# Packed attention and a gated feed-forward on one core: the output product with its operands exchanged, and 64 leftover tokens of each batch kept for later

## The chip, the cores and the metric

The kernel runs on one core of a Trainium2 chip. The metric is the time of one execution on the device in microseconds (us). The core has a matrix engine (TensorE, PE in the profile; its weight loads are PEld), VectorE (DVE), ScalarE (ACT), GpSimd (POOL) and a queue engine (SyncE, SP) from which most transfers are issued. A matmul holds one operand in the array, the stationary one (up to 128 x 128, brought by a weight load), and streams the other, the moving one, column by column through it; its result lands in PSUM, which has eight banks of 512 float32 a partition.

## The reference

```python
# q, k, v: (8 batches, 8 heads, 576 tokens, 64); p: (8, 8, 32, 64)
def sm_attn(qq, kk, vv):
    s = 0.125 * qq @ kk.transpose(0, 1, 3, 2)
    a = np.exp(s - s.max(-1, keepdims=True))
    return (a / (a.sum(-1, keepdims=True) + 1e-9)) @ vv
packed = sm_attn(p, k, v)
attn = sm_attn(q, packed, packed)
x = attn.transpose(0, 2, 1, 3).reshape(4608, 512)
h = x @ w_in                      # w_in 512 x 2048, float64 in memory
g = h * erf(softplus(h))
out = g @ w_out                   # w_out 2048 x 512, float64 in memory
```

## The kernel before

Each batch of 576 tokens goes through attention, then through the feed-forward. The 2048 columns of w_in (rows of w_out) are 16 tiles f of 128. Large products are done in three terms with float32r operands split in a high and a low part: high x high, high x low, low x high.

**Attention** (`attention`, a generator of 12 stages) loads p, k, v, q, makes the first softmax a1 and the packed values pt, then the second softmax, whose high and low halves are `a2[b]`. The chunks of k, v and q share the `kvq` buffers (6 of 128 x 576). **W'** (`w_prime`, L248) multiplies pt with 512 columns of w_in, so that the h product runs from the softmax directly; tiles `wph` and `wpl`, four buffers each.

**Weights** arrive as float64: `load_f32` (L77) stages 128 x 512 words of 8 bytes in one of two buffers `wst` and converts them with one ACT and three DVE instructions (L88 to L91). The third to eighth of these loads borrow `wpl` and `wph` buffers (`EARLY`, L56). `split_w_out` makes the high and low part of each of the 16 w_out tiles.

**Units.** A unit before is (batch b, half c of its tokens, block i of two f tiles): 8 x 2 x 8 = 128 units. `h_block` (L284) computes two f tiles of h by 288 tokens, 12 matmuls with W' stationary and the 288 tokens moving (L297), copies them out of PSUM on ACT (L301, L303) and makes the gate. The first 32 units take softplus and erf in groups of three units with a table load on ACT for each (`gate_group`); the others use a formula of tanh and square on ACT (L311 to L316) and three DVE instructions (L314, L315, L317). `split_g` (L263) makes g's high and low part `gh`, `gl` on DVE (L266, L267), two buffers each. `o_block` (L323) then adds the unit's share of the output: 24 matmuls with 128 x 128 blocks of w_out stationary and 288 tokens of g moving (L337), into four banks `ps_o0` to `ps_o3`, one for each 128 output columns, holding the output transposed. At the end of a (batch, half) the banks are copied out on ACT (L344) and written to `outT`, which the host transposes.

**Order.** Batches 0 and 1 go through in two turns of eight f tiles each (`TURNS`), so that the second half of the weights may come later; their second turn adds to the output in memory by an accumulating transfer from POOL (L347). The loop at the end of the function emits, for each unit n, its h product, the items planned for n (attention stages, W', conversions), and the out product of unit n - 3 (`LAG`; n - 5 in the first 32). A scheduler with a simulated timeline then sets the order on each engine, where instructions run strictly in that order. Attention of batch 1 is planned over units 1 to 6, that of batch b + 2 over the first six units after batch b; each W' tile is planned as soon as a buffer of four is free.

Of the kernel before, what the change touches and what calls it, by code (L numbers as in the profile page):

```python
# [27 lines left out]
@with_exitstack  # L28
def tile_pack_attention_moe(ctx: ExitStack, tc: tile.TileContext, qT, kT, v, pT, w_in, w_out, outT):
    nc = tc.nc  # L30
# [4 lines left out]
    HT = S // 2  # L35
    NDM = DM // P
    FB = 512
    NFB = DFF // FB
    NBLK = DFF // (2 * P)
    NT = S // P  # L40
# [5 lines left out]
    G = 3  # L46
    GROUPED = 4 * NBLK
    LAG_G = 5
    NB0 = 2
    TURNS = (0, NBLK // 2, NBLK)  # L50
    WI_AT = (-1, 1)
# [73 lines left out]
    def attention(b, roomy=False):  # L125
# [5 lines left out]
        def chunk(name, tag="kvq"):  # L131
            if tag == "kvq":
                return apool.tile([P, S], F32, name=f"{name}_{b}", tag="kvq", bufs=6)[:]
            return tpool.tile([P, S], F32, name=f"{name}_{b}", tag=tag)[:]
# [18 lines left out]

        p = apool.tile([P, NC, NK], F32, name=f"p{b}", tag="p")
        nc.sync.dma_start(p[:], pT[b])
# [72 lines left out]
        blocks = ta[:].rearrange("p r (n k) -> p (r n) k", k=NK)  # L228
        mx = apool.tile([P, 4 * nb], F32, name=f"mx{b}", tag="mx")
        wide = mx[:].unsqueeze(2).to_broadcast([P, 4 * nb, NK])  # L230
# [31 lines left out]

    def split_g(hs, b, c, i):  # L263
        ghi = tpool.tile([P, 2, HT], F32R, name=f"gh{b}_{c}_{i}", tag="gh", bufs=2)
        glo = tpool.tile([P, 2, HT], F32R, name=f"gl{b}_{c}_{i}", tag="gl", bufs=2)
        nc.vector.tensor_copy(ghi[:], hs[:])  # L266
        nc.vector.tensor_tensor(glo[:], hs[:], ghi[:], op=ALU.subtract)  # L267
        gs[b, c, i] = (ghi, glo)

    def gate_group():  # L270

        ts = []
        for hs, b, c, i in group:
            t = tpool.tile([P, 2, HT], F32, name=f"t{b}_{c}_{i}", tag="t0")
# [4 lines left out]
        for t, (hs, b, c, i) in zip(ts, group):  # L279
            nc.vector.tensor_tensor(hs[:], t[:], hs[:], op=ALU.mult)  # L280
            split_g(hs, b, c, i)
        group.clear()

    def h_block(b, c, i, n):  # L284

        grouped = n < GROUPED
        hs = tpool.tile([P, 2, HT], F32, name=f"hs{b}_{c}_{i}", tag="t1" if grouped and n // G % 2 else "hs")
        for k in range(2):
            f = (2 * i + k) * P
            j, fo = f // FB, f % FB  # L290
            whi, wlo = wp[b, j]
            ps = ps_h.tile([P, 512], F32, name=f"h{b}_{c}_{i}_{k}", tag="ps_h")
            m = 0
            ahi, alo = a2[b]
            for r in range(2):
                for w, a in ((whi, ahi), (whi, alo), (wlo, ahi)):
                    nc.tensor.matmul(ps[:, 0:HT], w[:, r, fo:fo + P], a[:, r, c * HT:(c + 1) * HT],  # L297
                                     start=(m == 0), stop=(m == 5))
                    m += 1
            if grouped:  # L300
                nc.scalar.copy(hs[:, k, :], ps[:, 0:HT])  # L301
            else:
                nc.scalar.mul(hs[:, k, :], ps[:, 0:HT], 0.5)  # L303
        if grouped:
            group.append((hs, b, c, i))
            if len(group) == G or n == GROUPED - 1:
                gate_group()
            return
        t = tpool.tile([P, 2, HT], F32, name=f"t{b}_{c}_{i}", tag="t0")
        u = tpool.tile([P, 2, HT], F32, name=f"u{b}_{c}_{i}", tag="t1")  # L310
# [7 lines left out]
        split_g(hs, b, c, i)  # L318

    acc = {}  # L320
    begun = set()

    def o_block(b, c, i, first, last):  # L323

        g = gs.pop((b, c, i))
        t0 = b * S + c * HT
        if first:
            acc[b, c] = []
            for d in range(NDM):
                po = ps_o.tile([P, 512], F32, name=f"o{b}_{c}_{i}_{d}", tag=f"ps_o{d}")  # L330
                acc[b, c].append(po)
        for d in range(NDM):
            for k in range(2):
                f = 2 * i + k
                terms = [(wo_hi, g[0]), (wo_hi, g[1]), (wo_lo, g[0])]
                for n, (w, gg) in enumerate(terms):
                    nc.tensor.matmul(acc[b, c][d][:, 0:HT], w[f][:, d * P:(d + 1) * P], gg[:, k, :],  # L337
                                     start=(first and k == 0 and n == 0),
                                     stop=(last and k == 1 and n == len(terms) - 1))
        if not last:  # L340
            return
        for d in range(NDM):
            ob = tpool.tile([P, HT], F32, name=f"ob{b}_{c}_{i}_{d}", tag="ob", bufs=NDM)
            nc.scalar.copy(ob[:], acc[b, c][d][:, 0:HT])  # L344
            where = outT[d * P:(d + 1) * P, t0:t0 + HT]
            if (b, c) in begun:
                nc.gpsimd.dma_start(where, ob[:], accum_op=ALU.add)  # L347
            else:
                nc.sync.dma_start(where, ob[:])
        begun.add((b, c))  # L350


    segs = [(b, c, i0, i1) for i0, i1 in zip(TURNS, TURNS[1:]) for b in range(NB0) for c in range(2)]
    segs += [(b, c, 0, NBLK) for b in range(NB0, B) for c in range(2)]
    units = [(b, c, i, i == i0, i == i1 - 1) for b, c, i0, i1 in segs for i in range(i0, i1)]
    first_use, last_of, uses, last_use = {}, {}, [], {}
    for n, (b, c, i, _, _) in enumerate(units):
        first_use.setdefault(b, n)
        last_of[b] = n
        if (b, i // 2) not in last_use:  # L360
            uses.append((b, i // 2))
        last_use[b, i // 2] = n

# [6 lines left out]
    conv = {}  # L370
    for i in range(NBLK):
        ph = max(n for n, start in enumerate(TURNS) if i >= start)
        items = []
        if i % 2 == 0:
            items += [("wi", i // 2, c) for c in range(4)]
        items += [("wo", 2 * i), ("wo", 2 * i + 1)]
        conv.setdefault(ph, []).append(items)
    for ph, lists in conv.items():
# [4 lines left out]
        else:  # L383
            flat = [it for items in lists for it in items]
            n0, n1 = (2 * NB0 * TURNS[p] for p in (ph - 1, ph))
            for k, it in enumerate(flat):
# [19 lines left out]
    for k, (b, j) in enumerate(uses):  # L406
        if b not in ready:
            plan_attention(b)
        n = ready[b]
        if k >= NFB:  # L410
            n = max(n, last_use[uses[k - NFB]])
# [4 lines left out]
    for f in range(DFF // P):  # L416
        made = max(n for n, its in plan.items() if ("wo", f) in its)
# [39 lines left out]
    do(early[4:])  # L457
    behind = 0
    for n in range(len(units) + LAG):
        if n < len(units):  # L460
            grouping[0] = n < GROUPED
            h_block(*units[n][:3], n)
            do(plan.pop(n, []))
        while behind <= n - (LAG_G if n < GROUPED else LAG):
            o_block(*units[behind])
            behind += 1

# [37 lines left out]
```

## Time and profile before

| what | value |
|---|---|
| runs | 804.53, 797.12, 798.9 us; median 798.9 |
| profiled execution | span 795.2 us from the first to the last instruction; no separate time is given for it |
| TensorE busy | 742.5 us (93%), 6352 matmul instructions |
| weight loads busy | 669.1 us (84%) |
| DVE, ACT, POOL busy | 571.2 (72%), 582.7 (73%), 15.0 us (2%) |
| mean granted TensorE clock | 0.961 |
| transfers | 58.41 MB, mean 73 GB/s |

The matmuls are pipelined: the duration of one in the profile is its way through the array, and the distance between two starts is what it costs in a stream. The granted clock is given as a share of full speed. In a group's row, after the names and shapes and the count, stand the busy time in us, the mean duration of one in ns, and the idle time of the engine before them with what ended it.

### The profile page before, as it was taken

What the parts mean: (1) busy time and instruction counts of PE and PEld (TensorE: products, weight loads), DVE (VectorE), ACT (ScalarE), POOL (GpSimd) and SP (SyncE); (2) the same over time, 40 slices, a digit from 0 to 9 for tenths busy, and PEclk for the clock granted to TensorE, in tenths of its full rate; (3) what the DMA queues carried; (4) which work ended last, traced back from release to release, by engine and by line L of the source; (5) the groups of instructions that cost most, each with busy time, mean ns of one, the idle gap of its engine ahead of it and who ended that gap; (6) DMA issues with size and microseconds to landing.
All of it is one profiled execution on the core that took longest, in us unless ns stands there. A gap on an engine that the chain in (4) does not pass through costs nothing.

```text
span 795.2 us, 15330 instructions
## 1 busy us (share of the span) xinstructions
PE 742.5 (93%) x6352; PEld 669.1 (84%) x6352; DVE 571.2 (72%) x876; ACT 582.7 (73%) x974; POOL 15.0 (2%) x22
## 2 busy tenths in 40 slices
PE   3469858999999999999999999999999999999998
PEld 1248636899888899899888998899988999899998
DVE  3897787753386669767886769767786769776664
ACT  3368368868577778778687867888688877888784
POOL 0000000000111200000000000000000000000000
PEclk8559879999999999999999999999999999999999
DMA  9714633321441431002300221002400210000000
GB/s 312 279 58 154 216 130 114 102 65 48 106 87 13 94 84 57 31 2 82 132 31 1 82 76 57 32 1 79 132 31 1 70 54 2 31 1 31 2 31 31
DMA packets 31814, 58.41 MB, mean 73 GB/s; under 512 B 3584, under 2 KB 14848, under 8 KB 31744
## 3 DMA queue, kind: packets, MB, share of 16 engines
q1 hardware_dynamic: 29440, 55.06, 21.1%
q0 software_dynamic: 2304, 2.36, 2.4%
q8 instruction: 50, 0.82, 0.4%
q14 instruction: 20, 0.16, 0.1%
HBM read 45.61 MB, written 11.80 MB: 72 GB/s over the span
## 4 chain that ended last, share of the span: by engine, by line
PE 83%; ACT 6%; DVE 5%; DMA 5%; issue 1%; SPq 0%; ACTq 0%
PE o L337 49%; PE h L297 25%; PE wp L254 4%; PE p L209 2%; DMA wi<-w_in 2%; DMA q<-qT 1%; DMA wos<-w_out 1%; PE s L223 1%; PE s L176 1%; PE t L197 1%; ACT t L275 1%; ACT L278 1%; ACT t L278 1%; ACT a L185 1%; DMA p<-pT 1%
## 5 line engine op out<-in xcount | busy, mean ns | idle before, releaser
L337 PE MATMUL o<-gh,woh 128*128 128x288 f32 x1024 | 301.4, 301 | 4.0 <-ACT woh L104 2.9
L337 PE MATMUL o<-gl,woh 128*128 128x288 f32 x1024 | 301.6, 296 | 0.6 <-DVE gl L267 0.6
L337 PE MATMUL o<-gh,wol 128*128 128x288 f32 x1024 | 300.7, 296 | 0.0
L337 PEld LDWEIGHTS o<-gh,woh 128*128 128x128 f32 x1024 | 190.3, 188 | 32.8 <-DVE t L314 8.1
L337 PEld LDWEIGHTS o<-gh,wol 128*128 128x128 f32 x1024 | 192.5, 189 | 6.4 <-issue 6.0
L337 PEld LDWEIGHTS o<-gl,woh 128*128 128x128 f32 x1024 | 192.9, 188 | 1.3 <-DVE gl L267 0.9
L297 PE MATMUL h<-a2h,wph 128*128 128x288 f32 x512 | 155.2, 304 | 15.7 <-ACT a2h L243 10.4
L297 PE MATMUL h<-a2l,wph 128*128 128x288 f32 x512 | 154.4, 302 | 2.2 <-DVE a2l L244 2.2
L297 PE MATMUL h<-a2h,wpl 128*128 128x288 f32 x512 | 154.5, 302 | 0.4 <-DVE wpl L257 0.4
L303 ACT ACTIVATE hs<-h 128x288 f32<-128x288 f32 x192 | 78.1, 412 | 80.3 <-PE h L297 77.2
L297 PEld LDWEIGHTS h<-a2h,wph 128*128 128x128 f32 x512 | 98.5, 193 | 27.6 <-ACT a2h L243 13.9
L317 DVE SCALAR_TENSOR_TENSOR hs<-t,hs 128x576 f32<-128x576 f32 x96 | 72.5, 755 | 60.4 <-ACT t L316 60.4
L297 PEld LDWEIGHTS h<-a2h,wpl 128*128 128x128 f32 x512 | 99.0, 193 | 3.4 <-issue 2.7
L297 PEld LDWEIGHTS h<-a2l,wph 128*128 128x128 f32 x512 | 98.8, 193 | 3.4 <-DVE a2l L244 2.9
L267 DVE TENSOR_TENSOR gl<-hs,gh 128x576 fp32r<-128x576 f32 x128 | 96.4, 753 | 1.9
L266 DVE CAST gh<-hs 128x576 fp32r<-128x576 f32 x128 | 58.4, 456 | 47.5 <-PE o L337 46.3
L316 ACT ACTIVATE t<-t,bias 128x576 f32<-128x576 f32 x96 | 74.0, 771 | 23.0 <-DVE t L315 22.7
L314 DVE SCALAR_TENSOR_TENSOR t<-t,hs 128x576 f32<-128x576 f32 x96 | 71.8, 748 | 13.0 <-ACT u L313 12.8
L311 ACT ACTIVATE t<-hs,bias 128x576 f32<-128x576 f32 x96 | 74.5, 776 | 2.2
L312 ACT ACTIVATE t<-t,bias 128x576 f32<-128x576 f32 x96 | 74.3, 774 | 1.9
L313 ACT ACTIVATE u<-t,bias 128x576 f32<-128x576 f32 x96 | 74.5, 776 | 1.5
L315 DVE SCALAR_TENSOR_TENSOR t<-u,t 128x576 f32<-128x576 f32 x96 | 72.3, 753 | 1.2
(65 smaller groups left out, 661.8 us busy)
## 6 DMA issues: line engine op xcount, KB each, us to landing
k<-kT SPq DMA_DIRECT2D x32, 288.0 KB, 4.3
q<-qT SPq DMA_DIRECT2D x32, 288.0 KB, 4.3
outT<-ob SPq DMA_DIRECT2D x64, 144.0 KB, 1.8
wi<-w_in SPq DMA_DIRECT2D x16, 512.0 KB, 5.9
v<-v SPq DMA_DIRECT2D x32, 256.0 KB, 3.6
wos<-w_out SPq DMA_DIRECT2D x16, 512.0 KB, 4.1
outT<-ob POOLq DMA_DIRECT2D x16, 144.0 KB, 4.5
v<-v SPq DMA_DIRECT2D x8, 128.0 KB, 4.5
```

The costliest lines, as they stand in the source:

```text
L266: nc.vector.tensor_copy(ghi[:], hs[:])
L267: nc.vector.tensor_tensor(glo[:], hs[:], ghi[:], op=ALU.subtract)
L297: nc.tensor.matmul(ps[:, 0:HT], w[:, r, fo:fo + P], a[:, r, c * HT:(c + 1) * HT], start=(m == 0), stop=(m == 5))
L303: nc.scalar.mul(hs[:, k, :], ps[:, 0:HT], 0.5)
L311: nc.scalar.activation(t[:], hs[:], AF.Tanh, bias=bias[:, 0:1], scale=2.0 * T_SCALE)
L312: nc.scalar.activation(t[:], t[:], AF.Square, bias=bias[:, 1:2], scale=Q_SCALE)
L313: nc.scalar.activation(u[:], t[:], AF.Tanh, bias=bias[:, 2:3], scale=U_SCALE)
L314: nc.vector.scalar_tensor_tensor(t[:], t[:], 0.5 * A2, hs[:], op0=ALU.mult, op1=ALU.add)
L315: nc.vector.scalar_tensor_tensor(t[:], u[:], 0.5 * A1, t[:], op0=ALU.mult, op1=ALU.add)
L316: nc.scalar.activation(t[:], t[:], AF.Tanh, bias=bias[:, 3:4], scale=2.0 * A_SCALE)
L317: nc.vector.scalar_tensor_tensor(hs[:], t[:], 1.0, hs[:], op0=ALU.add, op1=ALU.mult)
L337: nc.tensor.matmul(acc[b, c][d][:, 0:HT], w[f][:, d * P:(d + 1) * P], gg[:, k, :], start=(first and k == 0 and n == 0), stop=(last and k = ...
```

## The change

The operands of the output product change places. For each f tile and each 128 tokens of a batch, g's 128 x 128 block is now stationary and 512 columns of w_out are moving, so the result is 128 tokens by all 512 output columns, a full bank, no longer transposed. A unit is one f tile by the whole batch of 576 tokens: still 128 units, with 12 h matmuls and the same gate on 128 x 576. 576 tokens are four tiles of 128 and 64 left over. `split_g` copies the 64 left tokens of gh and gl on GpSimd into tiles kept for a pair of batches (`rest`: 4 f tiles x 2 batches x 64 tokens each), and `o_rest` computes them as one full tile of 128 tokens after the pair's second batch: 4 groups of 12 matmuls in bank `ps_o0`. For the last pair these groups are put between and behind the last units' out products, in a bank of attention. A unit's first out product takes the banks in the order 1, 2, 3, 0.

To make room, `kvq` has five buffers instead of six, p and mx one instead of two, W' three instead of four, the borrowed staging buffers (`EARLY`) are four instead of six; `ob` has three of 128 x 512 instead of four of 128 x 288. The turns of batches 0 and 1, the lags, the planned units of attention and of the conversions keep their numbers; with the new units, a W' tile is used by four units in a row and f tile n is needed at unit n of a turn, where before two were needed at each of the first four units.

```diff
-    opool = ctx.enter_context(tc.tile_pool(name="wo", bufs=2 * (DFF // P) + 1))
+    opool = ctx.enter_context(tc.tile_pool(name="wo", bufs=2 * NF + 1))
...
-    EARLY = ("wpl", "wpl", "wph", "wph", "wpl", "wpl")
+    EARLY = ("wpl", "wpl", "wph", "wph")
...
-    wpool = ctx.enter_context(tc.tile_pool(name="wp", bufs=NFB))
+    rpool = ctx.enter_context(tc.tile_pool(name="rest", bufs=NFB))
+    wpool = ctx.enter_context(tc.tile_pool(name="wp", bufs=NW))     # NW = 3
...
+        pair, k = b // 2, f // PER
+        if (pair, k) not in rest:
+            rest[pair, k] = [rpool.tile([P, PER, 2, TAIL], F32R, name=f"{x}{pair}_{k}", tag=x) for x in ("rh", "rl")]
+        for kept, g in zip(rest[pair, k], (ghi, glo)):
+            nc.gpsimd.tensor_copy(kept[:, f % PER, b % 2, :], g[:, NTB * P:S])
...
+    def terms(g, f):
+        return ((g[0], wo_hi[f]), (g[1], wo_hi[f]), (g[0], wo_lo[f]))
+
+    def o_block(b, f, first, last):
+        g = gs.pop((b, f))
+        order = range(NTB)
+        if first:
+            order = [*range(1, NTB), 0]
+            acc[b] = [ps_o.tile([P, 512], F32, name=f"o{b}_{f}_{x}", tag=f"ps_o{x}") for x in range(NTB)]
+        for x in order:
+            for n, (gg, w) in enumerate(terms(g, f)):
+                nc.tensor.matmul(acc[b][x][:], gg[:, x * P:(x + 1) * P], w[:], start=(first and n == 0),
+                                 stop=(last and n == 2))
+        if not last:
+            return
+        for x in range(NTB):
+            ob = tpool.tile([P, DM], F32, name=f"ob{b}_{f}_{x}", tag="ob", bufs=3)
+            nc.scalar.copy(ob[:], acc[b][x][:])
...
+    def o_rest(pair, k):
+        if k == 0:
+            if pair == B // 2 - 1:
+                acc["rest"] = ps_m.tile([P, 2, 512], F32, name=f"or{pair}", tag="ps_m")[:, 0, :]
+            else:
+                acc["rest"] = ps_o.tile([P, 512], F32, name=f"or{pair}", tag="ps_o0")[:]
+        g = rest.pop((pair, k))
+        for i in range(PER):
+            for n, (gg, w) in enumerate(terms(g, k * PER + i)):
+                nc.tensor.matmul(acc["rest"], gg[:, i].rearrange("p two t -> p (two t)"), w[:],
+                                 start=(k == 0 and i == 0 and n == 0),
+                                 stop=(k == NFB - 1 and i == PER - 1 and n == 2))
...
+    stream = []
+    for n, (b, f, _, last) in enumerate(units):
+        stream.append((n, o_block, units[n]))
+        if b % 2 and f == NF - 1 and b < B - 1:
+            stream += [(n, o_rest, (b // 2, k)) for k in range(NFB)]
+    for k, back in enumerate((3, 2, 2, 1)):
+        at_n = max(i for i, it in enumerate(stream) if it[0] == len(units) - back)
+        stream.insert(at_n + 1, (len(units) - back, o_rest, (B // 2 - 1, k)))
```

More of the change, by code (lines that the diff above doesn't have):

```diff
@@ L28, in tile_pack_attention_moe @@
 @with_exitstack
-def tile_pack_attention_moe(ctx: ExitStack, tc: tile.TileContext, qT, kT, v, pT, w_in, w_out, outT):
+def tile_pack_attention_moe(ctx: ExitStack, tc: tile.TileContext, qT, kT, v, pT, w_in, w_out, out):
     nc = tc.nc
@@ L132, in chunk @@
             if tag == "kvq":
-                return apool.tile([P, S], F32, name=f"{name}_{b}", tag="kvq", bufs=6)[:]
+                return apool.tile([P, S], F32, name=f"{name}_{b}", tag="kvq", bufs=5)[:]
             return tpool.tile([P, S], F32, name=f"{name}_{b}", tag=tag)[:]
@@ L278, in gate_group, with h_block @@
             in_turn(nc.scalar.activation(t[:], t[:], AF.Erf))
-        for t, (hs, b, c, i) in zip(ts, group):
+        for t, (hs, b, f) in zip(ts, group):
             nc.vector.tensor_tensor(hs[:], t[:], hs[:], op=ALU.mult)
-            split_g(hs, b, c, i)
+            split_g(hs, b, f)
         group.clear()
-    def h_block(b, c, i, n):
+    def h_block(b, f, n):
         grouped = n < GROUPED
[L287 to L292, printed above, removed]
+        hs = tpool.tile([P, S], F32, name=f"hs{b}_{f}", tag="t1" if grouped and n // G % 2 else "hs")
+        j, fo = f // PER, f % PER * P
+        whi, wlo = wp[b, j]
+        ahi, alo = a2[b]
+        for c in range(2):
+            at_c = slice(c * HT, (c + 1) * HT)
+            ps = ps_h.tile([P, 512], F32, name=f"h{b}_{f}_{c}", tag="ps_h")
             m = 0
-            ahi, alo = a2[b]
             for r in range(2):
                 for w, a in ((whi, ahi), (whi, alo), (wlo, ahi)):
-                    nc.tensor.matmul(ps[:, 0:HT], w[:, r, fo:fo + P], a[:, r, c * HT:(c + 1) * HT],
-                                     start=(m == 0), stop=(m == 5))
+                    nc.tensor.matmul(ps[:, 0:HT], w[:, r, fo:fo + P], a[:, r, at_c], start=(m == 0), stop=(m == 5))
                     m += 1
             if grouped:
-                nc.scalar.copy(hs[:, k, :], ps[:, 0:HT])
+                nc.scalar.copy(hs[:, at_c], ps[:, 0:HT])
             else:
-                nc.scalar.mul(hs[:, k, :], ps[:, 0:HT], 0.5)
+                nc.scalar.mul(hs[:, at_c], ps[:, 0:HT], 0.5)
         if grouped:
-            group.append((hs, b, c, i))
+            group.append((hs, b, f))
             if len(group) == G or n == GROUPED - 1:
@@ L317, in h_block @@
         nc.vector.scalar_tensor_tensor(hs[:], t[:], 1.0, hs[:], op0=ALU.add, op1=ALU.mult)
-        split_g(hs, b, c, i)
+        split_g(hs, b, f)
     acc = {}
     begun = set()
-    def o_block(b, c, i, first, last):
-        g = gs.pop((b, c, i))
-        t0 = b * S + c * HT
-        if first:
[L328 to L339, printed above, removed]
+    def terms(g, f):
[3 more added lines that the diff above has]
+        order = range(NTB)
+        if first:
+            order = [*range(1, NTB), 0]
[4 more added lines that the diff above has]
+                                 stop=(last and n == 2))
         if not last:
             return
[L342 to L346, printed above, removed]
+        for x in range(NTB):
+            ob = tpool.tile([P, DM], F32, name=f"ob{b}_{f}_{x}", tag="ob", bufs=3)
+            nc.scalar.copy(ob[:], acc[b][x][:])
+            where = out[b * S + x * P:b * S + (x + 1) * P, :]
+            if b in begun:
                 nc.gpsimd.dma_start(where, ob[:], accum_op=ALU.add)
@@ L349, in o_block @@
                 nc.sync.dma_start(where, ob[:])
[L350 to L355, printed above, removed]
+        begun.add(b)
+    def o_rest(pair, k):
[10 more added lines that the diff above has]
+                                 stop=(k == NFB - 1 and i == PER - 1 and n == 2))
+        if k < NFB - 1:
+            return
+        ob = tpool.tile([P, DM], F32, name=f"obr{pair}", tag="ob", bufs=3)
+        nc.scalar.copy(ob[:], acc["rest"])
+        for x in range(2):
+            t0 = (2 * pair + x) * S + NTB * P
+            nc.sync.dma_start(out[t0:t0 + TAIL, :], ob[x * TAIL:(x + 1) * TAIL, :])
+    segs = [(b, f0, f1) for f0, f1 in zip(TURNS, TURNS[1:]) for b in range(NB0)]
+    segs += [(b, 0, NF) for b in range(NB0, B)]
+    units = [(b, f, f == f0, f == f1 - 1) for b, f0, f1 in segs for f in range(f0, f1)]
     first_use, last_of, uses, last_use = {}, {}, [], {}
-    for n, (b, c, i, _, _) in enumerate(units):
+    for n, (b, f, _, _) in enumerate(units):
         first_use.setdefault(b, n)
         last_of[b] = n
-        if (b, i // 2) not in last_use:
-            uses.append((b, i // 2))
-        last_use[b, i // 2] = n
+        if (b, f // PER) not in last_use:
+            uses.append((b, f // PER))
+        last_use[b, f // PER] = n
     def at(n):
@@ L370, in tile_pack_attention_moe @@
     conv = {}
-    for i in range(NBLK):
-        ph = max(n for n, start in enumerate(TURNS) if i >= start)
+    for i in range(NF // 2):
+        ph = max(n for n, start in enumerate(TURNS) if 2 * i >= start)
         items = []
@@ L409, in tile_pack_attention_moe @@
         n = ready[b]
-        if k >= NFB:
-            n = max(n, last_use[uses[k - NFB]])
+        if k >= NW:
+            n = max(n, last_use[uses[k - NW]])
         n = max([n] + [m for m, its in plan.items() if any(it[0] == "wi" and it[1] == j for it in its)])
@@ L414, in tile_pack_attention_moe @@
         whole_w[b] = n
-    for f in range(DFF // P):
+    for f in range(NF):
         made = max(n for n, its in plan.items() if ("wo", f) in its)
@@ L461, in tile_pack_attention_moe @@
             grouping[0] = n < GROUPED
-            h_block(*units[n][:3], n)
+            h_block(*units[n][:2], n)
             do(plan.pop(n, []))
-        while behind <= n - (LAG_G if n < GROUPED else LAG):
-            o_block(*units[behind])
-            behind += 1
+        while stream and stream[0][0] <= n - (LAG_G if n < GROUPED else LAG):
+            _, block, what = stream.pop(0)
+            block(*what)
 def kernel(**inputs):
```

41 lines of the change are left out of this document (22 added, 19 removed).

## The prediction, made before the changed kernel was run

> **What bounds the kernel now.** I read the page's head first, then the windows before and after 140 us, then the chain and the timeline of TensorE.
>
> ```profile
> span 795.2 us, 15330 instructions
> ...
> PE 742.5 (93%) x6352; PEld 669.1 (84%) x6352; DVE 571.2 (72%) x876; ACT 582.7 (73%) x974; POOL 15.0 (2%) x22
> ```
>
> The page gives a span and no separate time. The median of the three runs shown, 798.9 us, lies 3.7 us above the span; I work on the span and add 3.7 at the end. The windows cut the span in two (columns: stretch, its length, then busy time and count of each engine, granted TensorE clock, DMA share, GB/s):
>
> ```profile
> 0.00:140.00 140.00, 92.39 (x754) 70.08 (x755) 102.44 (x175) 82.22 (x136) 0.70 (x6) 0.78 0.54 180
> 140.00:795.20 655.20, 650.08 (x5600) 599.06 (x5599) 468.81 (x702) 500.44 (x839) 14.27 (x16) 1.00 0.18 51
> ```
>
> After 140 us TensorE is busy 650 of 655 us at full granted clock, while ACT has 500 and DVE 469: TensorE's stream sets the end. Before 140 us it is busy 92 of 140 at a mean clock of 0.78, so there others set the pace. The same windows for the out product alone (line 337; here the columns after the length are PE, PEld):
>
> ```profile
> 0.00:140.00 140.00, 31.04 (x192) 27.78 (x193) 0.78 0.54 180
> 140.00:795.20 655.20, 411.86 (x2880) 389.45 (x2880) 1.00 0.18 51
> ```
>
> A unit has 24 out matmuls, so 192 are 8 units, and 2880 are the other 120 of 128. The chain in order of time (start, us, what) gives a unit's price in the full stretch:
>
> ```profile
> 405.45 3.20 PE o L337 x24
> 408.65 1.60 PE h L297 x12
> ```
>
> 3.20/24 = 133.3 ns from one out matmul to the next, and 1.60/12 = 133.3 for the h product, which has the same shape, 128x128 by 288 columns.
>
> **What 288 columns cost and what 512 will.** In columns nothing is saved: before 3072 x 288 = 884,736, after (8 batches x 16 f x 4 tiles + 4 pairs x 16 f) x 3 terms = 1728 matmuls x 512 = 884,736. All depends on what a matmul costs beside its columns. First the timeline of the matmuls at half clock, then at full clock (the duration in column 2 holds the pipeline's latency; the cadence is the distance of the starts):
>
> ```profile
> 46.04 0.45 PE L297 MATMUL h<-a2h,wph 128*128 128x288 f32 x1
> 46.28 0.45 PE L297 MATMUL h<-a2l,wph 128*128 128x288 f32 x1
> ...
> 160.44 0.29 PE L337 MATMUL o<-gh,woh 128*128 128x288 f32 x1
> 160.56 0.29 PE L337 MATMUL o<-gl,woh 128*128 128x288 f32 x1
> ```
>
> At half clock the cadence is 0.24 us, 0.833 ns a column; at full clock the columns alone would then take 120 ns, and 133.3 is 13.3 more. At half clock there is no room left for a fixed addition. So I ask what the weight loads do at both clocks:
>
> ```profile
> 45.39 0.29 PEld L297 LDWEIGHTS h<-a2l,wph 128*128 128x128 f32 x1 [2.03 <-DVE a2l L244]
> ...
> 46.28 0.33 PEld L297 LDWEIGHTS h<-a2h,wpl 128*128 128x128 f32 x1
> ```
>
> ```profile
> 187.66 0.19 PEld L337 LDWEIGHTS o<-gh,woh 128*128 128x128 f32 x1 [0.81 <-ACT ob L344]
> ...
> 406.09 0.19 PEld L337 LDWEIGHTS o<-gl,woh 128*128 128x128 f32 x1
> ```
>
> The first of each pair meets an idle array, the second runs in the stream. At half clock the load is stretched from 0.29 to 0.33: it waits for the matmul in front. At full clock it is 0.19 both times: it waits for nothing, begins when the matmul before begins, and the next matmul waits for it. I read 133.3 ns as the load's own cycle, a floor under the matmul and not an addition. The 0.12 us step from 160.44 to 160.56 shows that 288 columns can pass nearly at 120 ns.
>
> For 512 columns the bounds are: columns alone, 512 x 0.4167 = 213.3 ns; the 13.3 added, 226.7; 133.3 scaled by columns, 237.0. I take 216, columns and a few ns, since the half-clock rows and the unstretched load speak for the floor; 226.7 and 237 stay in the range.
>
> The Trainium skill, "TensorE: Matmul & The Clock Gate", section "LDWEIGHTS (loading the stationary operand)", puts a load at columns/1.2 ns, an estimate of 106.7 here. That is below 120, so by it the load is hidden already and the 13.3 would be something else that stays at 512 columns: this speaks for 226.7, not 216. The 133.3 of the chain is not explained by it; the rows decide.
>
> **The sum in the full stretch.** Out product of the 120 units after 140 us: 120 x 3.20 = 384.0. After: 120 x 12 x 0.216 = 311.0, and the kept tokens' 4 x 4 x 12 = 192 matmuls, all late, 41.5. Together 352.5, so **-31.5 us**. By 226.7: 326.4 + 43.5 = 369.9, -14.1. By 237: 341.3 + 45.5 = 386.8, +2.8. The h product keeps its 1536 matmuls of 288 columns and its order of weights matters not: 0.
>
> **Do ACT and DVE follow?** Half a batch without and with attention (8 units each):
>
> ```profile
> 400.46:442.64 42.18, 42.18 (x345) 39.01 (x351) 32.32 (x46) 34.54 (x56) 0.00 (x0) 1.00 0.04 15
> 442.64:491.24 48.60, 48.27 (x459) 43.11 (x459) 36.84 (x59) 36.08 (x63) 0.00 (x0) 1.00 0.28 88
> ```
>
> Eight units of out product go from 25.6 to 8 x 12 x 0.216 = 20.7 us, so the halves shrink to 37.3 and 43.7, with ACT at 34.5 and DVE at 36.8: 93% and 84%. All four W' products of a batch fall in the first of these halves; with a W' tile used by four units in a row they spread over both, which eases it. TensorE stays the bound, with a third of the former slack. A unit's output chain has three units of lag (LAG), now 3 x (1.60 + 2.59) = 12.6 us instead of 14.4. Evictions and the DVE rows:
>
> ```profile
> L267 DVE TENSOR_TENSOR gl<-hs,gh 128x576 fp32r<-128x576 f32 x128 | 96.4, 753 | 1.9
> L266 DVE CAST gh<-hs 128x576 fp32r<-128x576 f32 x128 | 58.4, 456 | 47.5 <-PE o L337 46.3
> ...
> L344 ACT COPY ob<-o 128x288 f32<-128x288 f32 x80 | 29.1, 398 | 4.8 <-PE o L337 4.8
> ...
> L337 PE MATMUL o<-gh,woh 128*128 128x288 f32 x1024 | 301.4, 301 | 4.0 <-ACT woh L104 2.9 <-ACT ob L344 1.0
> ```
>
> 80 evictions of 288 become 40 + 4 of 512, each between 398 and 398 x 512/288 = 708 ns; I take 0.6, so 26 us of ACT instead of 29: 0. But at each of the 3 pair ends in mid-run the kept tokens' product needs the bank ps_o0, which ACT must first evict behind its queue, and at 9 segment changes the first out matmuls need the other three, with three ob buffers where there are four evictions, so that the fourth waits for a transfer. TensorE has the next h product as cover; without it a wait is an ACT copy or two, 0.4 to 1.4 us. Twelve places: 0 to 17 us, and I take **+4**, near the low end, because all of today's changes together cost the out matmuls 1.0 us of waiting for an eviction (last row). Where no h product stands in the 48 matmuls (10.4 us), ACT and DVE run dry, but TensorE does not, and the lag refills behind it: 0.
>
> **GpSimd.** Each unit adds two copies of 128x64 on POOL. The trace has no such copy; its nearest rows are:
>
> ```profile
> L347 POOL DMA_DIRECT2D outT<-ob x16 | 14.3, 1061 | 263.1 <-ACT ob L344 256.9 <-ACT hs L301 3.1 <-ACT hs L303 2.1
> masks.py:199 POOL TENSOR_SCALAR_AFFINE_SELECT ident<-ident 128x128 f32<-128x128 f32 x1 | 0.3, 288 | 0.1
> ```
>
> Bounds 0.1 to 1.06 us; half the elements of the 288 ns row: 0.2 to 0.3. They gate only the reuse of gh and gl two units later, so 0. The accumulating output DMAs of the second half of batches 0 and 1 wait on POOL for ACT's eviction, and the copies queue behind them; then a cast (L266) is late, twice, by a few us inside the lag: 0 to 3, in the +4. The Trainium skill, "SBUF — State Buffer", section "🔬 SBUF: two separate sides", has GpSimd and DVE take a shared port pair in turn for whole instructions, also when DVE reads two SBUF inputs as L267 does. No row here shows it; it is priced as a rival below.
>
> **The start.** The chain before 140 us:
>
> ```profile
> 82.66 3.40 DMA wos<-w_out
> ...
> 89.39 5.17 DMA wos<-w_out
> ...
> 95.62 4.63 PE o L337 x33
> ...
> 114.73 1.37 DVE a2l L244
> 116.15 2.78 PE h L297 x10
> ```
>
> TensorE stands still until w_out tiles 6 and 7 are converted, since unit 3 uses them today; then attention of batch 1 goes on, and its a2l frees the h product at 116. With one f a unit, unit 3 needs tile 3 only: that can take out up to 95.6 - 82.7 = 12.9 us. Against it: EARLY lends the loads four buffers instead of six, so two conversions more go through the two-deep staging, and with five kvq buffers a v load of batch 0 and a q load of batch 1 start later on SP, with the loads behind them. Two turns of the staging at the 5.17 us transfer each are 10.3 us if nothing covers them. DVE, 102 of 140 us busy, does the same conversions either way and lies under both. Bounds -12.9 and +10.3, I take 0.
>
> Sum: -31.5 + 4 + 0 = -27.5; span 767.7, and with 3.7 the run takes **771 us**. At the end, the chain today has
>
> ```profile
> 779.35 12.78 PE o L337 x96
> ```
>
> the last four units' out product back to back. The last pair's kept tokens go between these, one group of 12 behind the last unit, and give its gate more cover, so nothing is lost there.
>
> **Rivals.**
> - The 13.3 ns are an addition. For it: the cadence is as steady as an added cost would make it. Against: half clock, and the 0.12 step. 795.2 - 14.1 + 4 + 3.7 = 789.
> - The change doesn't do what it says: the cost goes by columns, 237 ns. Against: the same. 795.2 + 2.8 + 4 + 3.7 = 806.
> - The start loses its 10.3 us instead of breaking even: 781. For: the stalls for w_out above. Against: half the tiles are needed per unit.
> - Slower: DVE becomes the bound through the POOL copies. A batch has 32.32 + 36.84 = 69.2 us of DVE in 90.8. With the copies locking DVE out, each in full, TensorE's new 81 us a batch (and 5 for kept tokens) is reached at (86 - 69.2)/32 = 0.52 us a copy, and the old 90.8 at 0.67. At 0.75 a batch takes 93.2, 2.4 more in each of 7.2: 795.2 + 17.3 + 3.7 = 816. Against: the 288 ns for twice the elements.
>
> **Chances.** Forecast 0.58, added cost 0.17, start 0.12, columns 0.06, DVE 0.07. A measurement here can tell about 1% from no change, so 791 to 807 is no change: faster 0.86, same 0.07, slower 0.07. The range reaches from a start that gains its 12.9 (758) with cheaper bank changes, 756, to 791, just past the added-cost case.
>
> **What would show it.** In the changed profile: 1728 out matmuls starting 0.21 to 0.22 us apart, loads of more than 0.19 in their stream (waiting again); h at 0.133 still; PE near full after the start with ACT's share up to 80%; idle before the kept tokens' first matmul of about a us; POOL copies under 0.3. It is wrong if the cadence is 0.227 or more, if ACT or DVE idle turns into PE idle in halves without attention, or if a2l of batch 1 ends later than 116 us.

## The result and the profile after

The changed kernel took 806.5 us in the median of four runs (805.5 to 807.4), the kernel before 798.6 beside it: a ratio of 1.010, with an interval of 1.006 to 1.014. The forecast was 771 and its range ended at 791. The profiled execution took 806.4 us, with a span of 804.6.

The head of the page after:

```profile
span 804.6 us, 12933 instructions
...
PE 742.4 (92%) x5008; PEld 579.1 (72%) x5008; DVE 575.8 (72%) x876; ACT 578.1 (72%) x938; POOL 132.2 (16%) x270
```

There are 1344 matmuls fewer, and TensorE is busy for the same time to 0.1 us. The window of after from 140 us on (columns as in those of before):

```profile
140.00:804.60 664.60, 657.89 (x4381) 524.02 (x4379) 474.14 (x703) 501.27 (x816) 121.39 (x248) 1.00 0.17 50
```

TensorE still sets the end (658 of 665 us busy), ACT and DVE lie at 75% and 71%. What a matmul costs is read from the chain of after, in order of time:

```profile
268.79 11.11 PE or L369 x48
...
405.12 2.74 PE o L345 x12
407.87 1.57 PE h L308 x12
409.44 1.02 PE wp L258 x16
```

That is 2.74/12 = 228.3 ns from one 512-column matmul to the next, with what a change to the h product costs, and 11.11/48 = 231.5 for the kept tokens. A stream by itself gives 226.7 in the next section; 227.5, between the two, is used below. The forecast went by 216.

The groups by form (count | busy us, mean ns | idle us before it, and what ended that), the W' group first as it was before, then the groups of after:

```profile
L254 PE MATMUL wp<-w_in_sb,pt 64*32 64x512 f32 x512 | 45.0, 632 | 10.1 <-DVE wpl L257 7.7 <-DVE ta L226 2.1 <-DVE w_in_sb L91 0.2
```

```profile
L345 PE MATMUL o<-woh,gh 128*128 128x512 f32 x512 | 173.1, 398 | 0.4 <-DVE gh L272 0.4
...
L369 PE MATMUL or<-woh,rh 128*128 128x512 f32 x64 | 25.2, 394 | 0.0
...
L258 PE MATMUL wp<-w_in_sb,pt 64*32 64x512 f32 x512 | 53.5, 679 | 18.5 <-DVE wpl L261 11.8 <-DVE ta L230 6.7
...
L279 POOL CAST rl<-gl 128x64 fp32r<-128x64 f32 x128 | 64.8, 507 | 116.6 <-DVE gl L273 91.4 <-PE or L369 25.2
```

The out product hardly waited for anything (0.4 us), the kept product not at all. The W' group is busy for 53.5 us where it was 45.0 before, for the same 512 matmuls. The POOL copies last half a us each, and not the 0.2 to 0.3 of the forecast. The sign that the forecast named for its floor, loads of more than 0.19 us in the new stream, did not come: they last 188 to 189 ns.

Where the 9.4 us of span came in is seen by putting the starts of the same unit's out product beside each other:

| first out matmul of unit | before, us | after, us | after minus before |
|---|---|---|---|
| 16 | 184.4 | 183.9 | -0.5 |
| 32 | 275.3 | 280.8 | +5.5 |
| 64 | 453.7 | 459.9 | +6.2 |
| 96 | 634.7 | 640.6 | +5.9 |
| last matmul | 791.8 | 798.1 | +6.3 |
| end of the span | 795.2 | 804.6 | +9.4 |

From unit 32 to the last matmul the two kernels run even (516.5 and 517.3 us), although 96 units of 12 x 227.5 ns and three pairs' kept tokens (3 x 11.11) cost 295.4 us where 96 x 3.20 = 307.2 stood: 12.6 us of the stream are lost again. (The spans are of one execution each. With the 1.8 us that lie outside the span, that of before is the execution of 797.1 us, its fastest; the medians differ by 8.0, not 9.4.) Three things had to be told apart: the cadence, which is the distance of two starts in a stream, that loss, and the start and tail. The ratios below are to the kernel before, each with its interval.

### The profile page after: what moved, and what is told of

It is laid out like the page before. It is cut to its first block, busy times and chain, and to the rows that moved or that the text cites. A ratio compares the mean times of both kernels' runs of the same rounds, so it can differ in the third digit from the quotient of the medians.

```text
span 804.6 us, 12933 instructions
## 1 busy us (share of the span) xinstructions
PE 742.4 (92%) x5008; PEld 579.1 (72%) x5008; DVE 575.8 (72%) x876; ACT 578.1 (72%) x938; POOL 132.2 (16%) x270
## 4 chain that ended last, share of the span: by engine, by line
PE 83%; DMA 6%; DVE 6%; ACT 4%; issue 1%; SPq 0%; DVEq 0%; ACTq 0%
PE o L345 42%; PE h L308 25%; PE or L369 5%; PE wp L258 5%; DMA wi<-w_in 2%; PE p L213 2%; DMA v<-v 2%; PE s L180 1%; PE s L227 1%; DMA wos<-w_out 1%; PE t L201 1%; DVE wo L94 1%; DVE wpl L261 1%; DVE wo L95 1%; DVE w_in_sb L94 0%
## 5 line engine op out<-in xcount | busy, mean ns | idle before, releaser
L345 PE MATMUL o<-woh,gl 128*128 128x512 f32 x512 | 201.2, 393 | 0.0
L345 PE MATMUL o<-wol,gh 128*128 128x512 f32 x512 | 200.7, 392 | 0.0
L345 PE MATMUL o<-woh,gh 128*128 128x512 f32 x512 | 173.1, 398 | 0.4 <-DVE gh L272 0.4
L308 PE MATMUL h<-a2h,wph 128*128 128x288 f32 x512 | 158.5, 310 | 12.3 <-ACT hs L311 8.3
L279 POOL CAST rh<-gh 128x64 fp32r<-128x64 f32 x128 | 61.7, 483 | 531.8 <-DVE gh L272 531.8
L308 PEld LDWEIGHTS h<-a2h,wph 128*128 128x128 f32 x512 | 97.8, 191 | 47.0 <-ACT hs L311 10.3
L345 PEld LDWEIGHTS o<-woh,gh 128*128 128x128 f32 x512 | 93.7, 189 | 29.7 <-issue 4.8
L345 PEld LDWEIGHTS o<-woh,gl 128*128 128x128 f32 x512 | 96.1, 188 | 21.1 <-DVE t L325 1.8
L345 PEld LDWEIGHTS o<-wol,gh 128*128 128x128 f32 x512 | 96.1, 188 | 20.3 <-issue 2.2
L273 DVE TENSOR_TENSOR gl<-hs,gh 128x576 fp32r<-128x576 f32 x128 | 101.0, 789 | 7.3 <-POOL rh L279 0.5
L279 POOL CAST rl<-gl 128x64 fp32r<-128x64 f32 x128 | 64.8, 507 | 116.6 <-DVE gl L273 91.4
```

The costliest lines, as they stand in the source:

```text
L279: nc.gpsimd.tensor_copy(kept[:, f % PER, b % 2, :], g[:, NTB * P:S])
L308: nc.tensor.matmul(ps[:, 0:HT], w[:, r, fo:fo + P], a[:, r, at_c], start=(m == 0), stop=(m == 5))
L345: nc.tensor.matmul(acc[b][x][:], gg[:, x * P:(x + 1) * P], w[:], start=(first and n == 0), stop=(last and n == 2))
```

## Experiments on the cadence and on the copies

**The matmul by itself.** A kernel that computes nothing of the reference: streams of 48 matmuls, one property varied in each.

```
one512..one128: b0[:, :n] += st[128x128, another each time].T @ mv[:, :n]   (float32r, n = 512, 448, 384, 288, 256, 128)
four_banks: into bank i % 4; same_weight: one block again; half_weight: a 128x64 block; bf512, bf288: bf16
```

> The disputed price by itself: streams of 48 matmuls, a new 128x128 float32r weight load before each, with 512, 448, 384, 288, 256 and 128 moving columns into one bank; then 512 columns spread over four banks, with one weight block loaded again and again, with a block of 64 columns, and bfloat16 operands. It computes nothing of the reference. Theory A (a fixed cost is added to the columns at full clock, as the changed kernel's 228 ns suggest): 227 at 512, 200 at 448, 173 at 384, 133 at 288, 120 at 256, 67 at 128. Theory B (the price goes by columns): 237, 207, 178, 133, 118, 59. Theory C (the forecast's floor under a load, and the changed kernel's 228 come from something around it): 216, 189, 162, 133, 133, 133. If the addition belongs to the weight load, 64 columns or bfloat16 at 512 make it smaller; if it belongs to the bank, four banks take it away and 512 falls to 216.

The chain of this kernel; L40, L44, L48, L52, L56, L60 are 512, 448, 384, 288, 256, 128 columns, L64 four banks, L68 one weight, L72 64 columns of weights, L76 and L80 bf16 with 512 and 288:

```profile
32.62 10.88 PE b L40 x48
43.50 8.16 PE b L64 x36
51.66 10.88 PE b L68 x48
62.54 11.04 PE b L72 x48
73.58 9.73 PE b L44 x48
83.31 8.32 PE b L48 x48
91.63 6.32 PE b L52 x48
97.95 5.75 PE b L56 x48
103.70 5.31 PE b L60 x48
109.01 10.37 PE b L76 x48
119.38 5.88 PE b L80 x48
```

Each divided by its count, all at full clock: 226.7, 202.7, 173.3 and 131.7 ns at 512, 448, 384 and 288 columns of float32r, that is the columns at 0.4167 ns and 11.7 to 16.0 on top of them, 13.3 at 512. Four banks (8.16/36) and one weight again give the same 226.7; a half block 230. At 128 columns, and only there, the matmul costs far more than that, 110.6 where 66.7 would follow: a floor. In bf16 it is 216.0 and 122.5, which is 2.7 and 2.5 on top. The groups of the same kernel show the loads, with 512 columns (L40), with a block of 64 columns (L72) and with 128 moving columns (L60):

```profile
L40 PEld LDWEIGHTS b<-mv,st 128*128 128x128 f32 x96 | 18.0, 188 | 3.7
...
L72 PEld LDWEIGHTS b<-mv,st 128*64 128x64 f32 x48 | 6.4, 134 | 4.5
...
L60 PEld LDWEIGHTS b<-mv,st 128*128 128x128 f32 x48 | 5.4, 192 | 0.0
```

A load lasts 192 ns in a stream with one every 110.6: its duration is no cycle, and the 0.19 us on which the forecast's floor rested bounds nothing. The load of 64 columns is shorter, 134 for 188 ns, and the matmuls do not come closer for it. So the 13.3 ns go with the type float32r and not with the length of the load; which step of a float32r matmul needs them is not shown, and no stream without loads was run.

**The bank.** Three matmuls in a row add to one bank; here four banks in turn.

```diff
-        for x in order:
-            for n, (gg, w) in enumerate(terms(g, f)):
+        for n, (gg, w) in enumerate(terms(g, f)):
+            for x in order:
```

> The changed kernel with the out product's loops exchanged: the three terms outside, the four token tiles inside, so that neighbouring matmuls go to different banks and share the moving block. If the 13 ns belong to adding again into the bank just written, 1536 matmuls lose 12 each: about 788 us. If they belong to the load or the stream, the time stays at 803 to 809.

808.8 us, 1.014 [1.013, 1.016]: not faster than the changed kernel. The time alone does not settle it, as the scheduler also issued W' in 33 pieces after unit 32 where the changed kernel has 27. The chain of this kernel does:

```profile
419.03 2.74 PE o L345 x12
```

Twelve matmuls cost 2.74 us as with one bank, so the order of banks is not what costs.

**Without the copies.** The kept tokens' product reads w_out blocks in place of g's 64 columns, and the copies on GpSimd are gone.

```diff
-        for kept, g in zip(rest[pair, k], (ghi, glo)):
-            nc.gpsimd.tensor_copy(kept[:, f % PER, b % 2, :], g[:, NTB * P:S])
```

> The changed kernel without the 256 GpSimd copies; the kept tokens' product takes blocks of w_out as its stationary operand in their place, so its 192 matmuls stay and the left tokens' rows are not the reference's. Theory 'copies are free': 803 to 808, since TensorE is full from 140 us on. Theory 'the copies hold DVE and the g buffers': DVE's gl falls from 789 to 753 ns and the time by 5 us or more, under 801.

809.2 us, 1.016 [1.014, 1.018]. DVE does get its time back, as the group of line 273 without the copies shows, and then with them:

```profile
L273 DVE TENSOR_TENSOR gl<-hs,gh 128x576 fp32r<-128x576 f32 x128 | 96.6, 755 | 2.4
```

```profile
L273 DVE TENSOR_TENSOR gl<-hs,gh 128x576 fp32r<-128x576 f32 x128 | 101.0, 789 | 7.3 <-POOL rh L279 0.5
```

That is 34 ns in each of 128 instructions, 4.4 us of DVE in the whole run, and the time did not fall with it. Two copies in the timeline of after, with the DVE instructions beside them:

```profile
337.27 0.24 POOL L279 CAST rh<-gh 128x64 fp32r<-128x64 f32 x1 [1.72 <-DVE gh L272]
337.31 0.81 DVE L273 TENSOR_TENSOR gl<-hs,gh 128x576 fp32r<-128x576 f32 x1
338.04 0.76 DVE L327 SCALAR_TENSOR_TENSOR hs<-t,hs 128x576 f32<-128x576 f32 x1
338.18 0.72 POOL L279 CAST rl<-gl 128x64 fp32r<-128x64 f32 x1 [0.68 <-DVE gl L273]
```

The first copy begins 0.04 us before the DVE instruction and takes 0.24; the DVE instruction takes 0.81 instead of 0.755. The second begins while a DVE instruction of two inputs runs and ends 0.10 after it. The Trainium skill, "SBUF — State Buffer", section "🔬 SBUF: two separate sides", has whichever of the two engines starts first keep a shared pair of ports for its whole instruction, and these rows agree. With 0.5 us for a copy on average, GpSimd waits more than DVE.

**Without the kept tokens' product.** It and the copies are left out; the 64 left rows of a batch get another block's data.

> The changed kernel without the copies and without the kept tokens' 192 matmuls; the left tokens' rows hold other data. If TensorE's stream sets the end, 192 x 0.229 = 44 us go: about 762 us. If ACT or DVE is next, less goes: their halves of a batch need 34.5 and 36.8 us before, so not under 790 when they bind by their sums plus waits. The start up to unit 12 should be as in the changed kernel.

756.8 us, 0.949 [0.948, 0.951]: 49.7 us less than the changed kernel, for 192 x 0.2315 = 44.4 us of TensorE's work. Of the other 5.3 the tail is 0.5; the scheduler also issued W' in fewer pieces here (21 after unit 32 for 27), and the next section shows what these cost. Work that leaves TensorE's stream leaves the end, so the stream is the bound.

## Experiments on the stream's pieces

W' and the score products (L258; L180 and L227) are small matmuls of 64 rows by 32 columns of the array, between float32r products on the whole of it. In the chain of after they are split into pieces:

```profile
676.15 0.99 PE wp L258 x8
...
678.13 0.99 PE wp L258 x6
...
682.88 0.97 PE wp L258 x2
```

A piece of 2 W' matmuls keeps TensorE for 0.97 us, as long as one of 16 (1.02, the row at 409.44 above). The timeline of the piece of 16 and of another place with a piece of 2:

```profile
409.37 1.09 PE L258 MATMUL wp<-w_in_sb,pt 64*32 64x512 f32 x16
```

```profile
226.92 0.40 PE L345 MATMUL o<-wol,gh 128*128 128x512 f32 x1
227.25 1.04 PE L258 MATMUL wp<-w_in_sb,pt 64*32 64x512 f32 x2
228.22 0.50 PE L345 MATMUL o<-woh,gh 128*128 128x512 f32 x1
228.56 0.40 PE L345 MATMUL o<-woh,gl 128*128 128x512 f32 x1
```

One W' matmul lasts 0.68 us in the mean (the group above), and yet all 16 are through in 1.09. The windows of line 258 in that piece (PE busy and, in brackets, the matmuls that run) show why:

```profile
409.36:409.43 0.07, 0.06 (x8) 0.06 (x13) 1.00 0.00 0
409.43:409.82 0.39, 0.39 (x8) 0.12 (x16) 1.00 0.00 0
```

Eight matmuls begin within 0.07 us and then run at the same time, each on a part of its own of the array (2 x 64 rows by 4 x 32 columns, as `w_prime` lays them out); the other eight follow as a second round. Each small product is two matmuls, one in each round, so a piece of 2 takes the two rounds that 16 take. A product that is split into two pieces is paid twice: that is the price of a piece, and not the change from one kind to the other. The change is seen at the edges: the out matmul before the piece of 2 costs 0.33 and the one behind it 0.34 instead of 0.23, some 0.2 together. After 140 us there are 37 pieces of W' and 33 of scores, before the change 32 and 25; from unit 32 to the last matmul 27 and 25, before the change 23 and 18.

**In one piece.** The order alone is changed: the scheduler is told to issue each W' product and each group of score matmuls together.

```diff
-                w_prime(it[1], it[2])
+                with tc.high_priority():
+                    w_prime(it[1], it[2])
```

and the same around the two loops of score matmuls.

> The changed kernel with the W' products and the two score products of attention at high priority, so that the scheduler leaves their 16 matmuls together: on TensorE W' comes in 32 pieces instead of 43, the scores in 33 instead of 39. Theory 'each piece costs a drain and a restart of about 0.55 us': 17 pieces fewer give 7 to 9 us, 798 or a little less. Theory 'a piece only shifts time that is waited elsewhere': 804 to 808.

796.2 us in 11 runs, 0.998 [0.997, 0.999]: 10 us come back. The chain of this kernel has W' whole again:

```profile
671.50 1.02 PE wp L260 x16
...
678.62 1.02 PE wp L260 x16
```

From unit 32 to the last matmul 20 and 20 pieces are left, 12 fewer (after 140 us 26 and 27, 17 fewer), and that stretch takes 505.2 us instead of 517.3, 12.1 less: 1.0 us a piece. W' busy in that stretch, before, after and in this kernel:

```profile
275.30:791.80 516.50, 24.89 (x320) 4.00 (x320) 1.00 0.14 45
```

```profile
280.80:798.10 517.30, 29.12 (x324) 4.52 (x320) 1.00 0.13 43
```

```profile
283.10:788.30 505.20, 21.78 (x320) 3.62 (x320) 1.00 0.13 44
```

With 40 pieces, about the 41 of before, the stretch is 11.3 us shorter than before the change, where the cadence alone gives 307.2 - 295.4 = 11.8. Unit 32 comes later (283.1 instead of 280.8), which takes 2.3 back.

**The same order in the kernel before.**

> The kernel before with the W' and score products at high priority, as the run with unsplit groups had it: on TensorE W' comes in 32 pieces instead of 39, the scores in 31 as before. If a piece costs about 0.55 us there as well, 7 pieces give 4 us: 794. If the loss of pieces belongs to the changed kernel's 512-column stream alone, no change: 796 to 799.

797.4 us in 12 runs, 1.000 [0.998, 1.001]. From unit 32 to the last matmul it gains 3.4 us (513.1 for 516.5), with 38 pieces there for 41: again about 1 a piece. But unit 16 comes at 191.0 instead of 184.4 and unit 32 at 280.6 instead of 275.3 in the profiled execution; by the medians the start lost what the stream gained. So the exchange of operands, with both kernels unsplit, is worth 513.1 - 505.2 = 7.9 us from unit 32 to the last matmul.

## Experiments on the start and the tail

The chain of after before 130 us, and the a2l of batch 1 in its timeline:

```profile
90.87 6.74 DMA wos<-w_out
```

```profile
120.33 1.35 DVE L248 TENSOR_TENSOR a2l<-tb,a2h 128x1152 fp32r<-128x1152 f32 x1
```

The wait for w_out stands where it stood before, up to 97.6 us instead of 95.6, and the a2l of batch 1 starts at 120.3 instead of 114.7. The 12.9 us that fewer early w_out tiles might have given did not come.

**Buffers taken from the kernel before.** First all of the change's economies except W' and ob, then two of them one by one.

```diff
-    EARLY = ("wpl", "wpl", "wph", "wph", "wpl", "wpl")
+    EARLY = ("wpl", "wpl", "wph", "wph")                 # in this and, alone, in the third
-        return apool.tile([P, S], F32, name=f"{name}_{b}", tag="kvq", bufs=6)[:]
+        return apool.tile([P, S], F32, name=f"{name}_{b}", tag="kvq", bufs=5)[:]   # in this and, alone, in the second
```

(p and mx have one buffer in the first alone.)

> The kernel before with three of the changed kernel's economies alone: EARLY with four entries, kvq with five buffers, p and mx with one. If these economies cost the start its 5.5 us whatever the out product does, this runs 4 to 7 us above the kernel before, about 803. If they cost something only in the new order of units, it runs within 2 us of the kernel before.

> The kernel before with kvq at five buffers instead of six, nothing else. If the lost 9 us of the three economies together come from kvq (loads of v and q of batch 1 late, its a2l after 120 us), this runs at 803 or more; if from the staging, at 797 to 800.

> The kernel before with four borrowed staging buffers instead of six, nothing else. The counterpart of the run with five kvq buffers: 803 or more if the staging carries the 9 us, 797 to 800 if kvq does.

All together 807.3 us, 1.012 [1.011, 1.014]; five kvq buffers alone 799.2, 1.002 [1.001, 1.003]; four borrowed staging buffers alone 805.0, 1.010 [1.008, 1.011]. In the kernel before, the two staging buffers are worth nearly 8 us: unit 16 comes at 192.2 instead of 184.4.

**Buffers given back to the changed kernel.** Two more staging buffers, once from the softmax tiles a2, once from the kept tokens' tiles, whose two halves are joined in one.

```diff
-    EARLY = ("wpl", "wpl", "wph", "wph")
+    EARLY = ("wpl", "wpl", "wph", "wph", "a2h", "a2l")   # the other kernel: "rr", "rr"
```

> The changed kernel with six borrowed staging buffers again: the fifth and sixth are the second buffers of a2h and a2l, which nothing else needs before attention of batch 1 is through. The changed kernel is 5.5 us behind at the end of batch 1 (unit 32 begins at 280.8 instead of 275.3 us). Theory 'staging': that lag goes, unit 32 begins at 275 to 277, and the time falls by 4 to 6 us to about 801. Theory 'the start is late for another reason' (the kvq buffers, or the scheduler's order): a2h of batch 0 stays near 46.9 us and the time at 804 to 808.

> The changed kernel with six staging buffers, the fifth and sixth now in the kept tokens' tiles (high and low part in one 4 KB tile, four of them; the third and fourth are first written after 160 us), so that a2h and a2l are left alone. Theory 'the start is late for want of staging': a2l of batch 1 near 115 us, unit 32 at 275 to 277, the time 800 to 802. Theory 'the start depends on the order that the scheduler finds, and no single buffer decides': a2l of batch 1 at 118 to 123, the time 804 to 810.

807.8 us, 1.013 [1.012, 1.014], and 808.9, 1.015 [1.013, 1.017]: neither is faster than the changed kernel. With the first, a2l of batch 0 is back at 43.3 us, but that of batch 1 starts at 122.0; with the second it starts at 118.8, and unit 32 comes at 283.5.

**The tail.** The timeline at the end of after:

```profile
796.66 1.56 ACT L351 COPY ob<-o 128x512 f32<-128x512 f32 x3 [3.36 <-PE o L345]
...
798.06 0.39 PE L369 MATMUL or<-wol,rh 128*128 128x512 f32 x1
799.39 0.58 ACT L351 COPY ob<-o 128x512 f32<-128x512 f32 x1 [1.17 <-DMA out<-ob]
800.18 0.58 ACT L375 COPY obr<-or 128x512 f32<-128x512 f32 x1 [0.20 <-DMA out<-ob]
```

Five copies go through three ob buffers, so the fourth and fifth wait for transfers: from the last matmul's start to the end it takes 6.5 us, where it was 3.4. This kernel puts those two in other buffers:

```diff
+            tag, bufs = ("hs", 3) if b == B - 1 and x == NTB - 1 else ("ob", 3)
...
+        ob = ... tag="t0" if pair == B // 2 - 1 else "ob"
```

> The changed kernel, with the fourth eviction of the last batch and that of the last pair's kept tokens in tiles of their own, so that they don't wait for an ob buffer's transfer. After the last matmul the changed kernel needs 6.5 us, the kernel before 3.4. If the wait is the cause: about 2 us less, 804. If the last transfers themselves take that long: no change, 806 to 807.

805.4 us, 1.009 [1.008, 1.011]: 1.1 less than the changed kernel, which the two intervals do not separate. In the profile the tail falls by 1.1, to 5.4, so the wait for buffers is 1.1 of the 3.1; the other 2 were not tested. This kernel also tells how far one execution can be trusted: all four engines run their instructions in the same order as in the changed kernel, and yet unit 32 comes at 284.4 us where it came at 280.8, while from there to the last matmul it takes 516.7 and 517.3. So a difference of some 3 us at the start may lie in the execution alone.

**Together.** The unsplit order and the tail's buffers are in all three of these; the first adds `v_at` (two v loads of batch 0 go to "t1" instead of kvq), the second the six staging buffers with "rr", the third both.

```diff
-        v_at = ("hs", "hs", "hs", "kvq", "kvq") if roomy else ("kvq",) * NCH
+        v_at = ("hs", "hs", "hs", "t1", "t1") if roomy else ("kvq",) * NCH
```

> The changed kernel with three mends: W' and scores unsplit, the last two evictions in tiles of their own, and the v chunks of batch 0 that shared kvq put into t1 buffers, so that batch 1 finds its kvq buffers as free as in the kernel before. The unsplit run is at 796; the tail gave 1 to 2. If kvq is what delays batch 1, its a2l comes before 118 us and the time is 789 to 792; if not, 793 to 796.

> The same six staging buffers with the unsplit groups and the mended tail. By the first theory 795 - 6 = about 789; by the second 793 to 798, with unit 32 still after 281 us. From unit 32 to the last matmul it should need 505 us either way, as the two unsplit runs did.

> The same again with batch 0's last v chunks outside kvq. First theory: 787 to 790. Second: 791 to 798, no better than without.

795.2 us, 0.997 [0.996, 0.998]; 796.4, 0.998 [0.997, 0.999]; and 790.1 (five runs, 789.6 to 792.0), **0.991 [0.990, 0.993]**: the last lies 0.9% below the kernel before. Its chain at the start:

```profile
113.56 1.35 DVE a2l L250
```

The a2l of batch 1 starts at 113.6 us (122.8 in the first, 117.0 in the second), unit 16 at 177.2, unit 32 at 276.2, and the last matmul at 783.1: 506.9 us for the stretch that took 516.5 before. Its last matmul comes 8.7 us before that of the kernel before: 9.6 are thus from the stream, and the start is 0.9 later.

What stays open: staging buffers and kvq relief bring the start back only together, and with other orders of the same work the start moved by up to 6.6 us (the kernel before, unsplit, at unit 16), of which some 3 may lie in the execution. How much is the buffers themselves and how much the order that the scheduler happens to find with them is not separated.

## Why the prediction was wrong, step by step

The forecast span was 767.7, measured 804.6: 36.9 us. By its own terms, at the measured rates, 120 x 12 x 0.2275 + 192 x 0.2315 = 372.0 us against the 384.0 of before:

| term | forecast | measured |
|---|---|---|
| out product after 140 us | -31.5 | -12.0 |
| bank changes, copies | +4 | about 0 |
| stream from unit 32 to the last matmul | 0, no term | +12.6 |
| start, to unit 32 | 0 | +5.7 |
| tail | 0 | +3.1 |
| sum | -27.5 | +9.4 |

(The start's 5.7 is the 5.5 of the table of units, and the 0.2 by which the new rate, with the first pair's kept product, ought to have been ahead there. The last column compares one execution of each kernel.)

**The cadence (19.5 of the 36.9).** The step that failed is "I read 133.3 ns as the load's own cycle, a floor". It rested on three readings. The load's 0.19 us is a way through and not a cycle, as the stream of 128 columns shows. The step of 0.12 us from 160.44 to 160.56 was one of many; the timeline of the kernel before goes on with

```profile
160.69 0.30 PE L337 MATMUL o<-gh,wol 128*128 128x288 f32 x1
160.83 0.29 PE L337 MATMUL o<-gh,woh 128*128 128x288 f32 x1
```

that is 0.13 and 0.14, and starts rounded to 0.01 us, one at a time, can't carry 13 ns. And from half clock, where 288 columns cost the columns alone, it doesn't follow that nothing is added at full clock. The Trainium skill, "TensorE: Matmul & The Clock Gate", section "Wait — 56ns, not 53.3ns?", says just that of a stream: columns alone at half clock, columns and some 2.5 ns at full clock. The 2.7 and 2.5 ns of the bf16 rows agree with it; float32r, with 13.3 at 512 columns, doesn't, and the measurement decides. The rival with 226.7 ns had the mechanism and the rate right to a ns. Its 789 missed the same later terms as the forecast.

**The pieces (12.6).** The prediction had no term for them: it moved W' in units ("spread over both, which eases it") and did not ask in how many pieces the scheduler would issue it. (Its reading that all four W' products fall in the first half of a batch was off too: 48 of the 64 matmuls do.) That splitting costs this is shown by the unsplit order, which brings back 12.1 us in the same stretch with the order alone changed. That the change splits the products more often is counted: 52 pieces in that stretch for 41. From each piece's first start to the next matmul of another product W' keeps TensorE there for 27.1 us instead of 23.3 and the scores for 17.0 instead of 13.1, 7.7 together, and 11 pieces with 0.2 at their edges make 2.2 more; some 3 of the 12.6 are not located, and 0.9 of these is only the choice of 227.5 over the chain's 228.3. Why the scheduler splits more often here was not tried.

**The start (5.7).** Its bounds of -12.9 and +10.3 held, the middle didn't. By the new rate unit 16 ought to be 8 x (3.20 - 2.73) = 3.8 us ahead and is 0.5: 3.3 us are lost until there. The other 2.4 are lost between units 16 and 32, behind the start itself, where W' takes 7.9 us of TensorE instead of 6.0, which is pieces again. The rival of a start that loses named the two staging turns. In the kernel before they cost 7.6 us (805.0); in the changed kernel the two buffers alone brought nothing back, so what its 3.3 us come from stays open.

**Bank changes and copies.** The 4 us were not spent: TensorE waited 0.4 us before out products. That the copies cost nothing was right, with a wrong size (0.5 us a copy for 0.2 to 0.3). The rival in which they make DVE the bound needed 0.52 us of DVE a copy; they took 34 ns of each gl instruction. (The chances of the three faster cases add up to 0.87, not 0.86; nothing hangs on it.)

**The tail (3.1).** "Nothing is lost there" looked at the gate's cover and not at what follows the last matmul: five evictions of 512 columns through three buffers. The buffers are 1.1 of it, the rest is not located.

**The time outside the span.** 1.8 us in every run here and not 3.7: the forecast set a median of runs beside one run's span. That is 1.9 us of the forecast's time.

Right were: TensorE stays the bound, ACT and DVE follow, h stays at 131 to 133 ns, the number of matmuls.

## What to carry to other kernels

When a product is re-tiled with the same number of columns, what there is to gain is the fixed cost of a matmul times the matmuls saved; measure that cost as the difference of two cadences at the same clock and in the same type, never from a duration. Where small products share the array side by side, count the pieces in which the scheduler issues them and not the matmuls: here a piece of two cost what one of sixteen did. A change that takes its room from staging buffers can pay for it at the start. And before a difference is explained from two profiles, see how far two executions in the same order lie apart in that stretch: here 3.6 us at the start and 0.6 in the stream.

## What the runs showed of the hardware

A float32r matmul of 128 x 128 weights costs its columns at full clock plus 13.3 ns at 512 columns, bf16 plus 2.7; bank, weight and half a block make at most 3.3 ns of difference. The eight small matmuls of a W' round (64 rows by 32 columns each) begin within 0.07 us and run at the same time, so a piece of 2 takes 0.97 us and one of 16 takes 1.02; at its edges a float32r matmul costs 0.33 and 0.34 us instead of 0.23. A 128x64 copy on GpSimd took 0.24 us when it began before a DVE instruction of two inputs, which then took 0.81 instead of 0.755, and 0.72 when it began during one, ending 0.10 after it.
